# Attention and Fourier mixing on one core: the last of seven products moved into the next unit, and a fourth PSUM bank for products, taken from the attention scores

## The chip, the core and the metric

The kernel runs on one core of one Trainium2 chip. The metric is the device time of one execution in microseconds (us). The engines are named as in the profile: PE (matmuls) with PEld (its weight loads), DVE (vector), ACT (scalar and activation), POOL and SP (which issues most DMAs). Matmuls write to PSUM, which here holds eight banks, each 128 partitions x 512 fp32 values; ACT and DVE read the banks and write results to the larger on-chip memory.

## The reference

Two independent parts share one output, `out[:, :1024]` and `out[:, 1024:]`, with S = 2048 rows and D = 1024:

```
qkv = x @ wqkv                        # 32 heads of 32
scores = q k^T * 32**-0.5             # key allowed when 0 <= query - key < 256
a = softmax(scores) v @ wo
b = dft_seq_re @ (x2 @ dft_hid_re^T) - dft_seq_im @ (x2 @ dft_hid_im^T)
out = concat([a, b], axis=-1)
```

All of it is fp32. The kernel splits each fp32 operand into two fp16 parts, high and low, and multiplies in three passes (high x high, high x low, low x high).

## The kernel before, in words

**Units of seven products.** Every large matrix product is cut into units of 2 x 2 blocks, and a unit is computed with seven block products instead of eight, from sums and differences of blocks (`seven`). One product is 12 matmuls with 512 columns (four K tiles, three passes; for V 24 with 256 columns), issued in groups of four (`mm`, line 674). The seven use three PSUM banks a, b, c in the order a b a c a b a. The sums run on inside a bank: after product 1, ACT copies bank a to bank c (line 1123), product 3 adds to a and product 4 to the copy in c, and so on. After each of the products 2 to 7 ACT or DVE reads the bank: `keep` and `add_out` (lines 1198, 1201) and `halves_out` (lines 394, 402) in the projections, `copy` and `add` (lines 1375, 1378) in the Fourier part and in the output projection. PE may go on in a bank only when that reading is done. Banks a and b change places from unit to unit.

**Stages.** First come units for Q, K and V of one half of the rows (up to about 276 us in the profile), then those of the other half. From then on the attention runs beside them (`attention`, a generator that `tick` advances as matmuls are recorded). From about 500 us to 1590 us the attention runs beside the Fourier part, which alternates eight "x" units (hidden transform, two plain products in a bank of their own each) with eight "c" units of seven products (sequence transform). The output projection with `wo` stands last, from about 1640 us, again in units of seven.

**Operands of a unit.** `seven_parts` makes the left operands: three tiles `st`, each with two of the parts (products 1 and 4, 3 and 5, 2 and 7), and one part in a spare place (product 6). ACT writes the high half (line 1035) and DVE the low (line 1036). There are four `st` tiles, taken in turn. Sums on POOL or DVE (line 1014) come before.

**Attention.** A step `s_step` handles 128 queries of two heads. PE computes their scores against at most three key blocks of 128 into a tile `S` (line 546), of which there are two, two banks each, a head in a bank. The oldest and the newest block share one mask: DVE copies, by a triangular predicate, the oldest block's scores over the newest block's (line 552), so only two blocks go on. DVE takes the row maximum (556), POOL makes a bias (563), ACT exponentiates (566), ACT and DVE split into `hl` (395, 399), a DMA transposes to `t`, POOL masks `z` and `t` (581, 584), and `v_step` multiplies with V into the one bank `pv` (616). The same bank `pv` serves small transposes that spread a maximum over the partitions (lines 434 and 997, read by DVE in lines 436 and 999).

**What sets the order.** All operations are recorded first, with a cost and the buffers that they read and write (`Plan.op`, `Ring`). `Plan.run` then places them with a list scheduler: on each engine, the ready operation with the earliest due time. A due time follows from the order of PE operations in the recording. Each engine executes its list in that fixed order. A `Ring` with n buffers lets buffer k be written when all operations on buffer k-n are done; a ring marked `free` gives its buffers to whoever comes first.

Of the kernel before, what the change touches and what calls it, by code (L numbers as in the profile page):

```python
# [10 lines left out]
F32 = mybir.dt.float32  # L11
# [9 lines left out]
P = 128  # L21
# [275 lines left out]
def c_mm(n):  # L297
    return max(0.032, n / 2400.0 + 0.0025)
# [3 lines left out]
def fused_kernel(ctx: ExitStack, tc: tile.TileContext, xa, wqk, wv, wo, xb, wd, cs, out):  # L302
# [51 lines left out]
    banks = [Ring(R, lambda k, t=t: ps_m.tile([P, CH], F32, tag=f"m{t}", name=f"m{t}_{k}"), 1) for t in range(3)]  # L354
    s_ring = Ring(R, lambda k: ps_s.tile([P, 2, 512], F32, tag="s", name=f"s_{k}"), 2)
# [53 lines left out]
    def dve(cost, fn, r=(), w=(), port=False):  # L409
        op("DVE", cost, fn, r=r, w=w, port=port)  # L410
# [20 lines left out]
    def scale_of(key, v, s, wk, down=2.0 ** -14):  # L431
        t1 = tops.pop(key)
        pt = pv_ring.new()
        op("PE", 0.26, lambda: nc.tensor.transpose(pt.t[:, :P], t1.t[:, 0:1].to_broadcast([P, P]), ident),
           r=[(t1, 0), "ident"], w=[pt])
        dve(0.285, lambda: nc.vector.tensor_reduce(v, pt.t[:, :P], axis=AX.X, op=ALU.max), r=[pt], w=[wk])
# [53 lines left out]
    def attention():  # L490
# [33 lines left out]
        def s_step(b):  # L524
# [6 lines left out]
            mats, cost, keys = [], 0.0, []  # L531
            for j in range(2):
                h = 2 * hp + j
                k0 = qb + 1 - nb
                while k0 <= qb:
                    k1 = min(qb + 1, (k0 // QB + 1) * QB)
                    at = (k0 - (qb - 2)) * P
                    ku, qu = k2s[g, k0 // QB], q2s[g, sc]
                    keys += [(u, x) for u in (ku, qu) for x in range(3)]
                    mats.append((j, at, at + (k1 - k0) * P, qu, h, ku, k0 % QB * P, k0 % QB * P + (k1 - k0) * P))  # L540
                    cost += c_mm((k1 - k0) * P) + 0.01
                    k0 = k1

            def run():
                for j, a, e, qu, h, ku, ka, ke in mats:
                    nc.tensor.matmul(S.t[:, j, a:e], qu.t[:, h, i * P:i * P + P], ku.t[:, h, ka:ke],  # L546
                                     start=True, stop=True, skip_group_check=True)

            op("PE", cost, run, r=sorted(set(keys), key=lambda k: (k[0].k, k[1])), w=[(S, 0), (S, 1)])
            w = min(nb, 2) * P  # L550
            sv = lambda: S.t[:, :, 3 * P - w:3 * P]
            dve(0.425, lambda: nc.vector.copy_predicated(S.t[:, :, 2 * P:3 * P], upper2,  # L552
                                                         S.t[:, :, :P] if nb == 3 else never2),
                r=["upper", "never"], w=[(S, 0), (S, 1)])
# [415 lines left out]
    wps = banks[2].new()  # L970
# [13 lines left out]
    def u_look(n):  # L984
# [11 lines left out]
        pt = pv_ring.new()  # L996
# [107 lines left out]
    def bank():  # L1104
        nb[0] += 1
        return banks[nb[0] % 3].new()
# [9 lines left out]
    def seven(q, mats, ev, hook):  # L1116
        ring = {"a": banks[q % 2], "b": banks[1 - q % 2], "c": banks[2]}
        bk = {r: ring[r].new() for r in "abc"}
        for pos in range(7):
            ps = bk["abacaba"[pos]]  # L1120
            mm(ps, mats(pos))
            if pos == 0:
                op("ACT", 0.58, lambda: nc.scalar.activation(bk["c"].t, bk["a"].t, AF.Copy), r=[bk["a"]], w=[bk["c"]])  # L1123
            else:
                ev[pos](ps)
            hook(pos)
# [45 lines left out]
    def sum_unit(n, kd, gp, pr, how):  # L1172
# [37 lines left out]
        nseven[0] += 1  # L1210
        seven(nseven[0], mats, ev, lambda pos: qhook(n, pos))

    nseven = [0]
# [56 lines left out]
    at(where["v", 0, 1] - 2, 1, wv_fetch)  # L1270
# [9 lines left out]
    s2 = spots.index((where["v", 0, 1] + 2, 1))  # L1280
# [90 lines left out]
    def pair_of_tiles(q, lhs, rhs, y1, y2, f, fk, out_y, hook):  # L1371
# [9 lines left out]
        def last2(ps):  # L1381
            add(y2, 0, ps)
            out_y(2 * q + 1, y2)

        def last1(ps):
# [4 lines left out]
              4: lambda ps: add(y2, 1, ps), 5: last2, 6: last1}  # L1390
        seven(q, lambda pos: four(lhs[pos], lambda h, k: rhs(pos, h, k), pos < 2), ev, hook)
# [30 lines left out]
    def hook(n, turn):  # L1422
        for f, args in todo.pop((n, turn), ()):
            f(*args)
# [13 lines left out]
    for n, (kind, p, c, i) in enumerate(units):  # L1438
        rate[0] = late_rate * (RX if kind == "x" else 1.0)
        if kind == "x":  # L1440
            x = uns.pop(n)
# [24 lines left out]
        def out_y(t, y, p=p, c=c):  # L1466
# [3 lines left out]
            else:  # L1470
# [4 lines left out]
              lambda f=f: f.t, [f], out_y, lambda turn: hook(n, turn))  # L1475
    for q in range(NT // 2):
# [10 lines left out]

    for r in att_rings.values():
        r.after = turn_first
# [55 lines left out]
```

## Time and profile before

| | us |
|---|---|
| median of 3 runs | 1820.83 (1820.69 to 1822.73) |
| the profiled execution | 1815.42 |
| its span, first to last instruction | 1813.4 |
| PE busy | 1713.3 (94%) |
| DVE busy | 1349.6 (74%) |
| ACT busy | 1085.7 (60%) |
| POOL busy | 825.7 (46%) |

The profile comes from one execution. Rows of the groups read: line, engine, operation, out<-in with shapes, count, then busy time, mean ns of one, and the engine's idle time before them with what ended it. In the table of waits a row reads: who waited <- for whom: us in total, times, longest. Matmuls overlap in a pipeline, so the mean duration of one is longer than the step from one to the next.

### The profile page before, as it was taken

What the parts mean: (1) busy time and instruction counts of PE and PEld (TensorE: products, weight loads), DVE (VectorE), ACT (ScalarE), POOL (GpSimd) and SP (SyncE); (2) the same over time, 40 slices, a digit from 0 to 9 for tenths busy, and PEclk for the clock granted to TensorE, in tenths of its full rate; (3) what the DMA queues carried; (4) which work ended last, traced back from release to release, by engine and by line L of the source; (5) the groups of instructions that cost most, each with busy time, mean ns of one, the idle gap of its engine ahead of it and who ended that gap; (6) DMA issues with size and microseconds to landing.
All of it is one profiled execution on the core that took longest, in us unless ns stands there. A gap on an engine that the chain in (4) does not pass through costs nothing.

```text
span 1813.4 us, 31174 instructions
## 1 busy us (share of the span) xinstructions
PE 1713.3 (94%) x11286; PEld 893.2 (49%) x11286; DVE 1349.6 (74%) x2246; ACT 1085.7 (60%) x1718; POOL 825.7 (46%) x1018
## 2 busy tenths in 40 slices
PE   6999999999999989999989999988889999999998
PEld 2447587674444445444444445444445444444443
DVE  8879996666887887776887776886666778667641
ACT  3435635556666767766777767686556777563322
POOL 0124401324535565525676666766564767612000
PEclk8999999999999999999999999999999999999999
DMA  5586799999996688886599999579899659775331
GB/s 220 180 292 239 255 310 274 269 222 221 225 251 145 149 208 195 201 206 144 97 194 207 197 210 200 124 137 186 156 174 213 151 117 170 151 192 105 105 93 70
DMA packets 461274, 337.89 MB, mean 186 GB/s; under 512 B 340800, under 2 KB 411456, under 8 KB 461120
## 3 DMA queue, kind: packets, MB, share of 16 engines
q1 hardware_dynamic: 454208, 310.74, 70.7%
q0 software_dynamic: 6912, 25.17, 8.0%
q8 instruction: 88, 1.44, 0.3%
q14 instruction: 66, 0.54, 0.1%
HBM read 173.95 MB, written 88.47 MB: 145 GB/s over the span
## 4 chain that ended last, share of the span: by engine, by line
PE 42%; DVE 18%; POOL 11%; ACT 10%; issue 10%; DMA 8%; SPq 0%; POOLq 0%; DVEq 0%; ACTq 0%
PE m L674 38%; POOL raw L1014 3%; POOL bias L563 3%; DMA t<-hl 3%; ACT s L566 3%; DVE top L420 2%; DVE st L1036 2%; PE pv L616 2%; DVE hl L399 2%; ACT st L1035 2%; DVE mx L556 2%; PE s L546 2%; POOL z L581 2%; ACT hl L395 1%; POOL t L584 1%
## 5 line engine op out<-in xcount | busy, mean ns | idle before, releaser
L674 PE MATMUL m<-reg,st 128*128 128x512 f16 x4680 | 1105.7, 380 | 32.6 <-ACT m L1123 12.2
L674 PEld LDWEIGHTS <-st 128*128 128x128 f16 x5448 | 515.4, 98 | 614.0 <-issue 65.4
L566 ACT ACTIVATE s<-s,bias,escs 128x256 f32<-128x256 f32 (+1 forms) x512 | 271.0, 530 | 242.6 <-POOL bias L563 229.9
L563 POOL TENSOR_SCALAR bias<-mx,escs 128x2 f32<-128x2 f32 x256 | 124.8, 487 | 358.9 <-DVE mx L556 278.1
L399 DVE TENSOR_TENSOR hl<-s,hl 128x512 f16<-128x512 f32 (+1 forms) x256 | 171.3, 670 | 132.9 <-ACT hl L395 131.3
L1014 POOL TENSOR_TENSOR raw<-raw,raw 128x512 f32<-128x512 f32 x128 | 182.3, 1425 | 184.3 <-DVE st L1036 171.5
L581 POOL TENSOR_SCALAR_AFFINE_SELECT z<-t 128x512 f16<-128x512 f16 x224 | 177.6, 795 | 80.4 <-DMA t<-hl 61.5
L584 POOL TENSOR_SCALAR_AFFINE_SELECT t<-t 128x512 f16<-128x512 f16 x224 | 172.0, 771 | 11.1
L556 DVE TENSOR_REDUCE mx<-s 128x2 f32<-128x512 f32 (+1 forms) x256 | 170.4, 668 | 5.5 <-DVE o L627 0.3
L1036 DVE SCALAR_TENSOR_TENSOR st<-raw,sc,st 128x1024 f16<-128x1024 f32 x96 | 134.0, 1401 | 33.9 <-ACT st L1035 32.1
L674 PEld LDWEIGHTS <-reg 128*128 128x128 f16 x1212 | 116.6, 98 | 72.7 <-issue 7.8
L395 ACT ACTIVATE hl<-s 128x512 f16<-128x512 f32 (+1 forms) x256 | 148.0, 580 | 3.1 <-DMA t<-hl 0.2
L546 PE MATMUL s<-qk,qk 96*128 96x128 f16 (+2 forms) x704 | 120.8, 276 | 14.4 <-DVE hl L399 13.5
L674 PE MATMUL m<-xz,st 128*128 128x512 f16 x576 | 131.7, 384 | 2.3 <-DVE ybig L402 0.8
L1035 ACT ACTIVATE st<-raw,sc 128x1024 f16<-128x1024 f32 x96 | 109.5, 1143 | 31.4 <-PE m L674 14.6
L674 PE MATMUL m<-reg 128*128 128x512 f16 x480 | 124.2, 384 | 3.6 <-ACT reg L1375 3.6
L616 PE MATMUL pv<-vt,t 128*128 128x65 f16 x1984 | 114.6, 186 | 4.6 <-POOL t L584 3.9
L552 DVE COPY_PREDICATED s<-upper,s 128x256 f32<-128x256 uint32 x224 | 94.0, 420 | 32.9 <-PE s L546 32.1
L616 PEld LDWEIGHTS <-t 128*128 128x128 f16 x1984 | 96.1, 97 | 36.0 <-issue 4.8
L616 PE MATMUL pv<-vt,z 128*128 128x65 f16 (+1 forms) x896 | 99.2, 186 | 8.1 <-POOL z L581 5.3
L546 PEld LDWEIGHTS <-qk 96*128 96x128 f16 x704 | 61.9, 98 | 75.8 <-DVE hl L399 18.1
L616 PEld LDWEIGHTS <-z 128*128 128x128 f16 x896 | 81.3, 97 | 32.5 <-POOL z L581 7.0
(156 smaller groups left out, 2130.6 us busy)
## 6 DMA issues: line engine op xcount, KB each, us to landing
raw<-in_cs_dram SPq DMA_DIRECT2D x64, 512.0 KB, 4.7
raw<-in_xb_dram SPq DMA_DIRECT2D x48, 512.0 KB, 5.3
qk<-qs SPq DMA_DIRECT2D x192, 128.0 KB, 3.8
out_dram<-ybig POOLq DMA_DIRECT2D x36, 512.0 KB, 7.9
qs<-ybig SPq DMA_DIRECT2D x64, 256.0 KB, 4.4
raw<-in_wd_dram SPq DMA_DIRECT2D x32, 512.0 KB, 4.9
raw<-in_wqk_dram SPq DMA_DIRECT2D x22, 512.0 KB, 5.6
vs<-ybig SPq DMA_DIRECT2D x32, 260.0 KB, 4.7
```

The costliest lines, as they stand in the source:

```text
L395: else nc.scalar.activation(dst(), src(), AF.Copy), r=r, w=w)
L399: op("DVE", c_dve(n), lambda: nc.vector.tensor_tensor(dst(), src(), hi(), op=ALU.subtract), r=r, w=w, port=port)
L546: nc.tensor.matmul(S.t[:, j, a:e], qu.t[:, h, i * P:i * P + P], ku.t[:, h, ka:ke], start=True, stop=True, skip_group_check=True)
L556: dve(c_dve(2 * w), lambda: nc.vector.tensor_reduce(mx.t, sv(), axis=AX.X, op=ALU.max, negate=True), r=[(S, 0), (S, 1)], w=[mx])
L563: op("POOL", 0.215, lambda: nc.gpsimd.tensor_scalar(bias.t, mx.t, es, PSHIFT, op0=ALU.mult, op1=ALU.add), r=[mx, ("esc", g // 2)], w=[bias])
L566: op("ACT", 0.32 + 0.00085 * w, lambda h=h: nc.scalar.activation(sv()[:, h], sv()[:, h], AF.Exp, bias=bias.t[:, h:h + 1], scale=es), r=[bi ...
L581: op("POOL", 0.637, lambda: nc.gpsimd.affine_select(out=z.t, in_=pk(), compare_op=ALU.is_gt, fill=0.0, base=0, pattern=[[0, 4], [-1, P]], ...
L584: op("POOL", 0.637, lambda: nc.gpsimd.affine_select(out=pk(), in_=pk(), compare_op=ALU.is_ge, fill=0.0, base=0, pattern=[[0, 4], [1, P]], ...
L616: nc.tensor.matmul(pvt()[:, r, j, lo:], lhs, vt.t[:, k % QB, at + lo:at + VW], start=a, stop=e, skip_group_check=True)
L674: nc.tensor.matmul(ps.t[:, j * n:j * n + n], lhs(), rhs(), start=first, stop=last, skip_group_check=True)
L1014: lambda: e.tensor_tensor(o(), a(), b(), op=ALU.subtract if sub else ALU.add), r=r, w=w, port=True)
L1036: op("DVE", c_dve(n, True), lambda: nc.vector.scalar_tensor_tensor(dst(1), src(), scl(), dst(0), op0=ALU.mult, op1=ALU.subtract), r=[*r, s ...
```

## The change

Each unit now uses banks in the order a b (a of the unit before) a b c a: products 1 and 2, then product 7 of the unit before (`flush`), then 3, 6, 4, 5. Product 7 is kept back as `last_of` until the next unit, so a unit's bank a lives into the next one and there are two banks a in turn. That makes four banks for products: two for a, one for b, one for c. Between two products in one bank stand two others, as recorded. In the Fourier part and the output projection the two additions into `y2` change places accordingly. `flush` is also called where the kind of work changes (before the second half, before "x" units, before and after the output projection).

The fourth bank comes from the scores. A tile `S` now is one bank and holds the two newer key blocks of both heads. The oldest block's scores go to a new bank `old`, of which there is one. The small transposes use `old` in place of `pv`. The score matmuls of a step become two recorded operations, `S` first, then `old`. The program has 352 more matmuls (11638 for 11286).

```diff
-    banks = [Ring(R, lambda k, t=t: ps_m.tile([P, CH], F32, tag=f"m{t}", name=f"m{t}_{k}"), 1) for t in range(3)]
-    s_ring = Ring(R, lambda k: ps_s.tile([P, 2, 512], F32, tag="s", name=f"s_{k}"), 2)
+    a_ring, b_ring, c_ring = (Ring(R, lambda k, t=t, n=n: ps_m.tile([P, CH], F32, tag=f"m{t + k % n}", name=f"m{t + k % n}_{k}"), n)
+                              for t, n in ((0, 2), (2, 1), (3, 1)))
+    old_ring = Ring(R, lambda k: ps_v.tile([P, CH], F32, tag="old", name=f"old_{k}"), 1, free=True)
+    s_ring = Ring(R, lambda k: ps_s.tile([P, 2, 2 * P], F32, tag="s", name=f"s_{k}"), 2)
...
     def scale_of(key, v, s, wk, down=2.0 ** -14):
-        pt = pv_ring.new()
+        pt = old_ring.new()
...
+            old = old_ring.new() if nb == 3 else None
...
+            n2 = min(nb, 2)
+            scores(lambda j, a, e: S.t[:, j, (2 - n2 + a) * P:(2 - n2 + e) * P], qb + 1 - n2, qb + 1, [(S, 0), (S, 1)])
+            if old is not None:
+                scores(lambda j, a, e: old.t[:, j * P:j * P + P], qb - 2, qb - 1, [old])
+            w = n2 * P
+            sv = lambda: S.t[:, :, 2 * P - w:2 * P]
+            dve(0.425, lambda: nc.vector.copy_predicated(
+                S.t[:, :, P:2 * P], upper2,
+                old.t[:, :2 * P].rearrange("p (j k) -> p j k", j=2) if nb == 3 else never2),
+                r=["upper", "never"] + ([old] if nb == 3 else []), w=[(S, 0), (S, 1)])
...
-        return banks[nb[0] % 3].new()
+        return (a_ring, b_ring, a_ring, c_ring)[nb[0] % 4].new()
...
-    def seven(q, mats, ev, hook):
-        ring = {"a": banks[q % 2], "b": banks[1 - q % 2], "c": banks[2]}
-        bk = {r: ring[r].new() for r in "abc"}
-        for pos in range(7):
-            ps = bk["abacaba"[pos]]
+    def flush():
+        if last_of[0] is not None:
+            last_of[0]()
+            last_of[0] = None
+
+    def seven(mats, ev, hook):
+
+        a, b, c = a_ring.new(), b_ring.new(), c_ring.new()
+        mm(a, mats(0))
+        op("ACT", 0.58, lambda: nc.scalar.activation(c.t, a.t, AF.Copy), r=[a], w=[c])
+        hook(0)
+        mm(b, mats(1))
+        ev[1](b)
+        hook(1)
+        flush()
+        hook(2)
+        for turn, (pos, ps) in enumerate(((2, a), (5, b), (3, c), (4, a))):
             mm(ps, mats(pos))
-            if pos == 0:
-                op("ACT", 0.58, lambda: nc.scalar.activation(bk["c"].t, bk["a"].t, AF.Copy), r=[bk["a"]], w=[bk["c"]])
-            else:
-                ev[pos](ps)
-            hook(pos)
+            ev[pos](ps)
+            hook(3 + turn)
+
+        def last():
+            mm(a, mats(6))
+            ev[6](a)
+
+        last_of[0] = last
...
-    at(where["v", 0, 1] - 2, 1, wv_fetch)
+    at(where["v", 0, 1] - 2, 3, wv_fetch)
...
     for n, (kd, gp, pr, how) in enumerate(plan):
         if n == half1:
+            flush()
...
         def last2(ps):
-            add(y2, 0, ps)
+            add(y2, 1, ps)
             out_y(2 * q + 1, y2)
...
-              4: lambda ps: add(y2, 1, ps), 5: last2, 6: last1}
+              5: lambda ps: add(y2, 0, ps), 4: last2, 6: last1}
...
         if kind == "x":
+            flush()
```

The scheduler decides what stands where. Three places in PE's list follow; tiles m0 to m3 are the product banks, and the rows left out at "..." are the weight loads and the other matmuls of a group of four. First, the output projection near the end, where product 5 has just ended in m0 and product 7 needs it. Before:

```order
L674 MATMUL m0_84_19998<-ext_18971,st_185_19885 128x512
L674 LDWEIGHTS raw_219_19767
L674 MATMUL m1_85_20042<-ext_18971,raw_219_19767 128x512
...
L674 LDWEIGHTS st_186_19922
L674 MATMUL m0_84_19998<-ext_18971,st_186_19922 128x512 [waits DVE_49]
```

The same place now, where product 7 of m0 follows groups of the next unit in m1 and m2:

```order
L683 MATMUL m0_96_20458<-ext_19552,st_183_20357 128x512
L683 LDWEIGHTS raw_218_20340
L683 MATMUL m1_97_20570<-reg2_82,raw_218_20340 128x512
...
L683 MATMUL m2_78_20586<-reg2_82,st_186_20526 128x512 [waits DVE_49]
...
L683 LDWEIGHTS raw_218_20340
...
L683 LDWEIGHTS st_184_20410
L683 MATMUL m0_96_20458<-ext_19552,st_184_20410 128x512 [waits DVE_49]
```

Before, one group of four matmuls stood between the two users of m0; now there are four groups, 16 matmuls.

Second, a turn from one c unit to the next. The tile st_102 takes the place of st_98 and is filled when the last product on st_98 has ended. Before, from that product to the first on st_102:

```order
L674 MATMUL m0_47_11496<-reg1_81,st_98_11434 128x512
...
L674 MATMUL m1_48_11576<-reg1_81 128x512
...
L674 MATMUL m0_47_11496<-reg1_81,st_99_11477 128x512 [waits DVE_49]
...
L674 MATMUL m1_49_11779<-reg1_81,st_100_11599 128x512 [waits DVE_49]
...
L674 MATMUL m0_48_11881<-reg1_81,st_102_11765 128x512 [waits Activation_49]
```

And now:

```order
L683 MATMUL m1_55_11648<-reg1_81,st_98_11646 128x512
...
L625 MATMUL pv_69_11971<-vt_18_11293,z_107_11933 128x65
...
L683 MATMUL m0_56_11948<-reg1_81,st_100_11870 128x512
...
L683 LDWEIGHTS st_102_11984 [waits Activation_49]
L683 MATMUL m2_45_12027<-reg1_81,st_102_11984 128x512
...
L683 LDWEIGHTS st_102_11984 [waits DVE_49]
```

Before, 28 matmuls of 512 columns and a PV step stood between the two; now it is 8 and a PV step.

Third, the scores around the same place. Before, both matmuls of a step and a transpose in `pv`:

```order
L546 LDWEIGHTS qk0_18_10965 [waits DVE_49]
L546 MATMUL s_147_11799<-qk1_20_11393,qk0_18_10965 128x384 [waits PE_49]
L546 LDWEIGHTS qk0_18_10965
L546 MATMUL s_147_11799<-qk1_20_11393,qk0_18_10965 128x384
L997 MATMUL pv_104_11804<-ident_85,topone_36_11712 128x128 [waits DVE_49,PE_49]
```

Now, with two steps' matmuls into `old`, the second of which waits for DVE to have read the first:

```order
L549 MATMUL s_145_12008<-qk1_20_11732,qk0_18_11380 128x256 [waits DVE_49]
...
L549 MATMUL old_145_12013<-qk1_19_11116,qk0_18_11380 128x128 [waits DVE_49]
...
L549 MATMUL old_146_12046<-qk1_20_11732,qk0_18_11380 128x128 [waits DVE_49]
...
L549 MATMUL s_146_12085<-qk1_20_11732,qk0_18_11380 128x256 [waits Activation_49]
```

One matmul of 384 columns has become one of 256 and one of 128 in another bank, and the step's two parts may stand in either order.

More of the change, by code (lines that the diff above doesn't have):

```diff
@@ L530, in s_step @@
             d = st[b] = {}
[L531 to L554, printed above, removed]
+            old = old_ring.new() if nb == 3 else None
@@ new lines, in scores, with run @@
+            def scores(dst, k0, k_end, w):
+                mats, cost, keys = [], 0.0, []
+                for j in range(2):
+                    h, k = 2 * hp + j, k0
+                    while k < k_end:
+                        k1 = min(k_end, (k // QB + 1) * QB)
+                        ku, qu = k2s[g, k // QB], q2s[g, sc]
+                        keys += [(u, x) for u in (ku, qu) for x in range(3)]
+                        mats.append((j, k - k0, k1 - k0, qu, h, ku, k % QB * P, k % QB * P + (k1 - k) * P))
+                        cost += c_mm((k1 - k) * P) + 0.01
+                        k = k1
+                def run():
+                    for j, a, e, qu, h, ku, ka, ke in mats:
+                        nc.tensor.matmul(dst(j, a, e), qu.t[:, h, i * P:i * P + P], ku.t[:, h, ka:ke],
+                                         start=True, stop=True, skip_group_check=True)
+                op("PE", cost, run, r=sorted(set(keys), key=lambda k: (k[0].k, k[1])), w=w)
@@ L968, in warm_up @@
         op("PE", n * 0.3, run, r=[("R", 40)], w=[ps])
-    wps = banks[2].new()
+    wps = c_ring.new()
     for i in range(4):
@@ L995, in u_look @@
         t1 = tops.pop(key)
-        pt = pv_ring.new()
+        pt = old_ring.new()
         op("PE", 0.26, lambda: nc.tensor.transpose(pt.t[:, :P], t1.t[:, 0:1].to_broadcast([P, P]), ident),
@@ L1209, in sum_unit @@
               6: lambda ps: plain_out(ps, 0, 1)}
-        nseven[0] += 1
-        seven(nseven[0], mats, ev, lambda pos: qhook(n, pos))
-    nseven = [0]
+        seven(mats, ev, lambda turn: qhook(n, turn))
     def x_piece(pr, r):
@@ L1279, in fused_kernel @@
             at(*spots[s1 + 2 * i + 3], scan_scale, key)
-    s2 = spots.index((where["v", 0, 1] + 2, 1))
+    s2 = spots.index((where["v", 0, 1] + 2, 3))
     for e in range(2):
@@ L1389, in pair_of_tiles @@
         ev = {1: lambda ps: copy(y2, 1, ps), 2: lambda ps: copy(y2, 0, ps), 3: lambda ps: copy(y1, 0, ps),
-              4: lambda ps: add(y2, 1, ps), 5: last2, 6: last1}
-        seven(q, lambda pos: four(lhs[pos], lambda h, k: rhs(pos, h, k), pos < 2), ev, hook)
+              5: lambda ps: add(y2, 0, ps), 4: last2, 6: last1}
+        seven(lambda pos: four(lhs[pos], lambda h, k: rhs(pos, h, k), pos < 2), ev, hook)
     todo = {}
@@ L1440, in fused_kernel @@
         if kind == "x":
+            flush()
             x = uns.pop(n)
@@ L1486, in fused_kernel @@
               lambda: fo, ["fo"], out_o, lambda turn: None)
+    flush()
     for r in att_rings.values():
```

2 lines of the change are left out of this document (added).

## The prediction

> **What bounds the kernel now.** I read the busy shares first, then the stretches, then who PE waited for, because the change moves PE's matmuls and who frees their banks.
>
> ```profile
> span 1813.4 us, 31174 instructions
> PE 1713.3 (94%) x11286; PEld 893.2 (49%) x11286; DVE 1349.6 (74%) x2246; ACT 1085.7 (60%) x1718; POOL 825.7 (46%) x1018
> ...
> PE 42%; DVE 18%; POOL 11%; ACT 10%; issue 10%; DMA 8%; SPq 0%; POOLq 0%; DVEq 0%; ACTq 0%
> ```
> ```profile
> 0.00:318.00 318.00, 294.58 (x1883) 181.59 (x1884) 268.17 (x348) 146.47 (x193) 71.58 (x87) 0.98 0.77 253
> 318.00:520.00 202.00, 196.54 (x1466) 113.39 (x1464) 151.98 (x274) 121.56 (x208) 76.55 (x118) 1.00 0.97 235
> 520.00:1590.00 1070.00, 1014.32 (x7002) 505.86 (x7000) 813.31 (x1496) 739.74 (x1221) 659.20 (x799) 0.99 0.84 172
> 1590.00:1813.00 223.00, 207.86 (x944) 92.41 (x942) 116.13 (x130) 77.96 (x99) 18.41 (x16) 0.99 0.44 115
> ```
> PE is busy 93 to 97% in every stretch (columns: PE, PEld, DVE, ACT, POOL, clock, DMA) at a granted clock of 0.98 to 1.00, no other engine above 85%. So time is won only where PE stands still, 100 us in all, and lost wherever PE is made to stand. These are the waits of PE (total us, times, longest):
>
> ```profile
> PE m L674 <- ACT m L1123: 14.4, 16, 2.0
> PE s L546 <- DVE hl L399: 13.5, 16, 1.7
> ...
> PE m L674 <- DVE ybig L1378: 7.5, 9, 3.5
> PE m L674 <- ACT ybig L1375: 6.4, 1, 6.4
> PE pv L616 <- POOL z L581: 5.3, 2, 4.1
> PE m L674 <- DVE late L1378: 4.3, 5, 1.5
> ...
> PE pv L616 <- POOL t L584: 3.9, 6, 1.6
> PE pv L997 <- DVE o L627: 3.7, 4, 2.1
> PE m L674 <- ACT reg L1375: 3.6, 1, 3.6
> PE m L674 <- ACT reg L1198: 3.3, 3, 1.9
> PE m L674 <- DVE reg L1201: 2.8, 5, 0.8
> PE m L674 <- DVE ybig L402: 2.4, 6, 0.5
> PE m L674 <- ACT ybig L394: 1.6, 1, 1.6
> PE pv L616 <- DVE vwd L436: 1.3, 2, 1.0
> PE m L674 <- DVE st L1036: 1.3, 3, 0.6
> PE pv L616 <- DVE o L627: 1.3, 3, 0.8
> ...
> PE m L674 <- DVE reg L1378: 1.0, 3, 0.4
> PE pv L616 <- DVE sc L999: 0.8, 3, 0.4
> ...
> PE pv L434 <- DVE sc L999: 0.3, 1, 0.3
> ```
> Ten of these rows (m behind L1123, L1375, L1378, L1198, L1201, L402 and L394) are one thing: a product wants a bank that ACT or DVE has not finished reading. They sum to 47.3 us in 50 waits. One such place, near the end:
>
> ```profile
> 1746.69 1.03 PE L674 MATMUL m<-ext,st 128*128 128x512 f16 x4
> ...
> 1747.55 1.03 PE L674 MATMUL m<-ext,raw 128*128 128x512 f16 x4
> ...
> 1748.06 1.23 DVE L1352 TENSOR_TENSOR late<-raw 128x1024 f32<-128x1024 f16 x1 [8.63 <-DMA raw<-ots]
> ...
> 1749.20 1.40 DVE L1378 SCALAR_TENSOR_TENSOR late<-m,fo,late 128x512 f32<-128x512 f32 x2
> 1749.99 1.02 PE L674 MATMUL m<-ext,st 128*128 128x512 f16 x4 [1.42 <-DVE late L1378]
> ```
> Four matmuls start every 0.86 us (1746.69 to 1747.55), 0.216 us each, yet are shown busy for 1.03: the last overhangs by 0.17. An idle time thus hides about 0.17 us of the delay, and the 50 waits cost 47.3 + 8.5 = 55.8 us. Here the evicting add stood behind another DVE instruction that waited for a DMA, and PE had only one group of four matmuls to run meanwhile.
>
> **1. Two products between users of a bank.** Counted over the whole order, each matmul at its step in the trace: of 500 turnarounds (a matmul needs a bank that ACT or DVE must first read) 255 have under 2.5 us of PE's work in between; in the changed kernel 100 of 499. The waits of the trace lie almost all in that class, since an eviction takes 0.58 to 0.75 us and the rest is its queue. If those that stay close wait as often as now, 55.8 x 100/255 = 21.9 us stay and 33.9 us go. Upper end: all 55.8. Lower end: 20, because the two single waits of 6.4 and 3.6 us show ACT late by more than one further product (12 x 0.216 = 2.6 us) covers, and the shorter rows may lose less than their share. I take 34, the count being the nearest thing to a measurement. The copy of the first product into the third bank (16 waits, 14.4 us) is part of it: both its reader's wait and its writer now have two or more products.
>
> **2. The score bank.** The third key block goes to its own bank, of which there is one, and which the transposes of scales now use too. PE may write the next one only when DVE's masking copy has read the last.
>
> ```profile
> L552 DVE COPY_PREDICATED s<-upper,s 128x256 f32<-128x256 uint32 x224 | 94.0, 420 | 32.9 <-PE s L546 32.1
> ```
> The copy itself stays one of 0.42 us. The trace has no such bank; the nearest is the single bank pv, which DVE also frees and which PV steps and transposes share today. Its rows (L997 behind o, L616 behind vwd, o and sc, L434 behind sc) are 7.4 us in 13 waits, 9.6 us with the overhang, at 177 reuses of which 26 have under 2 us of PE's work between. After: pv has 7 such, the new bank 55 of 273. At 9.6/26 = 0.37 us each, 62 cost 22.9, so 13 us more than now. Ends: 10 us gained if none waits; 25 lost if half of the 62 wait at the 1.1 us that a bank wait costs today (55.8/50). I take 13. Behind a wait of PE here stand its products, and ACT and DVE behind those. The score tile keeps two buffers, so the 13.5 us behind the `hl` subtraction stay: counted from the later of both matmuls, reuses under 8 us go from 76 to 98, but those from 8 to 12 from 156 to 140.
>
> **3. Parts of a unit stay longer.** Product 7 reads the part that product 2 reads, and product 5, now the last before the next unit, the part that product 3 reads. There are four such tiles (`st`), so the next unit's second part is filled only after product 5, with little more than its first product to cover it.
>
> ```profile
> L1036 DVE SCALAR_TENSOR_TENSOR st<-raw,sc,st 128x1024 f16<-128x1024 f32 x96 | 134.0, 1401 | 33.9 <-ACT st L1035 32.1 <-POOL t L584 1.3
> ...
> L1035 ACT ACTIVATE st<-raw,sc 128x1024 f16<-128x1024 f32 x96 | 109.5, 1143 | 31.4 <-PE m L674 14.6
> ```
> A fill is 1.14 us on ACT and then 1.40 on DVE, 2.5 in a row. Of 185 refills 3 have under 5 us of PE's work between today, and 27 in the changed kernel, 16 of these under 4. PE waits for such a fill 1.3 us in all today. A close reuse of a bank costs 55.8/255 = 0.22 us now, and a fill passes two queues, so 0.44 x 24 = 10.5 us. Ends: 0, as the slack is still positive everywhere, and 26 (24 x 1.1). I take 10.5. The few units whose parts are loaded by SP's queue are in the 27. ACT's queue stands behind such a fill: exponentials wait there, but PE has two score tiles.
>
> **4. Shorter score matmuls.** The changed program has 352 more matmuls and weight loads in 176 blocks; columns stay the same.
>
> ```profile
> 1003.38 0.50 PE L546 MATMUL s<-qk,qk 96*128 96x128 f16 x4 [0.30 <-DVE hl L399]
> 1003.72 1.89 PE L674 MATMUL m<-reg,st 128*128 128x512 f16 x8
> ...
> 1009.78 0.50 PE L546 MATMUL s<-qk,qk 96*128 96x384 f16 x2 [0.71 <-DVE hl L399]
> 1010.11 0.20 PE L616 MATMUL pv<-vt,z 128*128 128x65 f16 x1
> ...
> L546 PEld LDWEIGHTS <-qk 96*128 96x128 f16 x704 | 61.9, 98 | 75.8 <-DVE hl L399 18.1
> ```
> A block in four matmuls (128 and 256 columns) takes 0.34 us to the next instruction, one in two of 384 takes 0.33. So 176 x 0.01 = 1.8 us. Lower end 0; upper end, if each of the 448 matmuls of 128 columns had to stand for its weight load (98 ns against about 55 by those 0.34 us), 19. I take 1.8, since the split block exists in the trace.
>
> The Trainium skill, "TensorE: Matmul & The Clock Gate", section "Back-to-back issue gap", gives a sustained spacing of about 81 ns for 128-column matmuls in a stream of load and matmul pairs. By that the 448 would take an estimated 11.6 us more than at 55 ns, and the sum would come out near no change. The trace does not agree: two matmuls of 256 and two of 128 in 0.34 us leave no room for 81.
>
> **5. Hooks, y tiles, ends.** Hooks keep seven places a unit; the fetch of the V weights moves from hook 1 to hook 3 of its unit, still two units ahead of its reader. Output tiles live about three products longer, four tiles against two a unit. Nothing for either. At the very end the last product follows its bank's last reader directly, as it does before.
>
> **Sum.** -33.9 + 13 + 10.5 + 1.8 = -8.6 us. Profiled: 1815.42 us, of which the span is 1813.4; the median of the runs, 1820.83, lies 5.4 above it, and I carry that over: span 1804.8, median 1812.
>
> **Rivals.** (a) The new waits stay covered, as the planner places other products in these gaps: terms 2 and 3 near 0, so -32 us and 1789. For it: the fills cause 1.3 us now; against: the gaps before were also placed by the planner and 50 of them failed. (b) Slower: the single score bank takes over. DVE is 76% busy from 520 to 1590 and works in order; with a 1.2 to 1.4 us fill ahead of the masking copy, PE stands. It decides from 0.56 us for each of the 62 close reuses (34.7 less 9.6 is 25 us, which with terms 3 and 4 outweighs the 33.9 by over 0.2%); at 0.7 us it is 33.8 lost, +12 and 1833. Against it: 0.37 in the nearest row. (c) Slower too: the late refill, 1.1 us at each of the 24: +7 and 1828. (d) Each 128-column matmul stands for its weight load: 19 for 1.8, +9 and 1830. Against it stands the 0.34 us; the section of the Trainium skill named under 4 speaks for a part of it. (e) No change: 55.7 of PE's 100 idle us lie between 520 and 1590 (1070.0 less 1014.3), where scores and masks follow a chain over four engines; if 9 us of what PE gains there become longer waits behind `hl`, `z` and `t` (22.7 us today), -8.6 becomes 0: 1821. That the order doesn't do what it says is excluded by the 255 and 100.
>
> **Chances.** Forecast 0.46, (a) 0.16, (e) 0.14, (b) 0.14, (c) 0.07, (d) 0.03. Three runs of this kernel spread by 0.1%, so 0.2% (3.6 us) is about what can be told from no change. Faster: 0.46 + 0.16 = 0.62; same 0.14; slower 0.24. The likeliest case alone has 1802 to 1817. The range runs from (a), 1789, to 1832, which takes in (c) and (d) and about half of (b).
>
> **What would show it.** Right: PE's waits for m behind ACT and DVE near 19 us (22 with overhang); waits of the new tile `old` and of pv together near 20; m behind `st` fills near 10; score blocks at 0.34 us; the stretches before 318 and after 1590, where no score bank exists and few refills are close, shorter by some 5 us each of the 23.4 and 15.1 us that PE idles there (318.0 less 294.58, 223.0 less 207.86). Wrong: bank waits that stay above 35 us (ACT and DVE late by more than two products), more than 35 us on `old` and pv, or waits behind `hl`, `z` and `t` that grow by more than 10.

## The result, and the profile after

| | before | after |
|---|---|---|
| median, us | 1820.76 (1819.67 to 1822.73) | 1771.78 (1766.37 to 1774.66) |
| profiled execution, us | 1815.42 | 1771.06 |

The two were run four times each on the same chip. The ratio is 0.9726, with a 95% interval of 0.9701 to 0.9751: the changed kernel is 49 us faster. The prediction said 1812 with a range of 1789 to 1832, so the direction was right and the size far off; the time lies 17 us below the range.

First the span, the busy times and the engines' shares of the chain of waits, in the profile of after:

```profile
span 1769.4 us, 31787 instructions
PE 1700.2 (96%) x11638; PEld 909.5 (51%) x11638; DVE 1347.5 (76%) x2246; ACT 1086.2 (61%) x1718; POOL 825.1 (47%) x1018
...
PE 56%; DVE 11%; POOL 10%; ACT 9%; issue 8%; DMA 6%; SPq 0%; POOLq 0%; DVEq 0%; ACTq 0%
```

The span fell by 44.0 us, PE's busy time by only 13.1 (1713.3 to 1700.2), and that of the other engines hardly: PE stands idle 69.2 us where it stood 100.1. In the chain, PE's share went from 42% to 56%, DVE's from 18% to 11%: the end is now set more by PE itself.

The same stretches of after (us, busy us of PE, PEld, DVE, ACT, POOL with counts, clock, DMA share, GB/s):

```profile
0.00:318.00 318.00, 299.32 (x1927) 185.55 (x1928) 269.19 (x351) 149.25 (x199) 73.60 (x89) 0.98 0.77 254
318.00:520.00 202.00, 199.97 (x1499) 117.22 (x1498) 157.69 (x280) 124.81 (x211) 75.90 (x115) 1.00 1.00 246
520.00:1590.00 1070.00, 1027.48 (x7419) 528.53 (x7416) 825.40 (x1512) 756.01 (x1237) 665.72 (x806) 1.00 0.85 178
1590.00:1769.00 179.00, 173.39 (x802) 78.21 (x800) 95.27 (x105) 56.09 (x74) 9.88 (x8) 0.99 0.38 97
```

PE's idle time is less in each: 18.7 us for 23.4 before 318, 2.0 for 5.5, 42.5 for 55.7 between 520 and 1590, and 5.6 for 15.1 after 1590, a stretch that now holds 802 matmuls for 944. The waits of PE (us in total, times, longest):

```profile
PE s L549 <- DVE hl L401: 16.3, 21, 2.0
...
PE m L683 <- ACT reg L1400: 4.7, 2, 3.6
PE pv L625 <- POOL t L593: 4.2, 5, 1.3
PE m L683 <- DVE st L1045: 4.1, 3, 1.8
PE m L683 <- ACT m L1136: 4.0, 8, 1.2
PE m L683 <- DVE reg L1227: 3.2, 3, 2.4
PE old L549 <- DVE s L560: 2.0, 2, 1.4
PE pv L625 <- POOL z L590: 1.8, 2, 1.6
PE pv L625 <- DVE o L636: 1.7, 4, 0.7
PE m L683 <- DVE ybig L1403: 1.3, 3, 0.7
...
PE m L683 <- ACT ybig L1400: 1.2, 1, 1.2
PE old L1006 <- DVE s L560: 0.8, 2, 0.4
PE m L683 <- DVE late L1403: 0.8, 1, 0.8
...
PE m L683 <- DVE reg L404: 0.5, 1, 0.5
PE old L549 <- DVE vwd L441: 0.5, 1, 0.5
PE old L436 <- DVE s L560: 0.4, 1, 0.4
...
PE pv L625 <- DVE sc L1012: 0.3, 1, 0.3
...
PE m L683 <- ACT reg L1224: 0.2, 1, 0.2
```

The rows of a product that wants its bank back (m behind L1400, L1136, L1227, L1403, L404, L1224) sum to 15.9 us in 20 waits, where there were 47.3 in 50. The waits of `old` and pv behind DVE sum to 5.7 us in 11; before, pv alone had 7.4 in 13. The refills of `st` cost 4.1 us in 3 waits, before 1.3 in 3.

**All of PE's lost time by cause.** The gaps alone don't sum to the 44 us. For every matmul I took the step from its start to the next matmul's start, less the ordinary step of its form (216 ns for 512 columns), and put the excess down to what released the next one; a slow step with no wait stands by itself. This counts the 0.17 us that a gap hides, and the slow clock. To see past the luck of one order, I averaged kernels that do equal work in another order, got by changing one cost constant of the scheduler (below): three of before, three with only the score side of the change, four of after. In us:

| what PE lost time to | before | score side only | after | after less before | predicted |
|---|---|---|---|---|---|
| bank of a product not read yet | 55.7 | 52.7 | 19.0 | -36.7 | -33.9 |
| slow matmuls without a wait | 21.4 | 13.3 | 12.8 | -8.6 | none |
| pv behind POOL's `z`, `t` | 13.0 | 4.4 | 7.4 | -5.6 | none |
| banks pv and `old` not read yet | 10.6 | 12.6 | 11.5 | +0.9 | +13 |
| parts and other operands late | 2.9 | 3.6 | 4.1 | +1.2 | +10.5 |
| scores behind `hl` | 18.7 | 20.4 | 21.2 | +2.5 | none |
| excess of short matmuls | 1.8 | 2.5 | 2.7 | +0.9 | +1.8 |
| mean span | 1817.0 | 1802.9 | 1773.1 | -43.9 | -8.6 |

The rows of the last column but one sum to -45.4; rows left out (the start, 13.9 us in each) make up the rest. The profiled execution of before lay 5.3 us under its median, that of after 0.7, which is why the medians differ by 49 and the profiled executions by 44.4.

### The profile page after: what moved, and what is told of

The parts are those of the page before. It is cut to its first block, busy times and chain, and to the rows that moved or that the text cites. A ratio compares the mean times of both kernels' runs of the same rounds, so it can differ in the third digit from the quotient of the medians.

```text
span 1769.4 us, 31787 instructions
## 1 busy us (share of the span) xinstructions
PE 1700.2 (96%) x11638; PEld 909.5 (51%) x11638; DVE 1347.5 (76%) x2246; ACT 1086.2 (61%) x1718; POOL 825.1 (47%) x1018
## 4 chain that ended last, share of the span: by engine, by line
PE 56%; DVE 11%; POOL 10%; ACT 9%; issue 8%; DMA 6%; SPq 0%; POOLq 0%; DVEq 0%; ACTq 0%
PE m L683 51%; POOL raw L1023 4%; ACT s L575 3%; POOL bias L572 2%; DMA raw<-in_cs_dram 2%; PE pv L625 2%; DVE hl L401 2%; DVE st L1045 2%; PE s L549 2%; POOL t L593 1%; DVE mx L565 1%; DMA t<-hl 1%; POOL z L590 1%; ACT hl L397 1%; ACT st L1044 1%
## 5 line engine op out<-in xcount | busy, mean ns | idle before, releaser
L683 PE MATMUL m<-reg,st 128*128 128x512 f16 x4680 | 1110.8, 379 | 14.1 <-ACT reg L1400 4.7
L572 POOL TENSOR_SCALAR bias<-mx,escs 128x2 f32<-128x2 f32 x256 | 129.0, 504 | 375.0 <-DVE mx L565 327.4
L1023 POOL TENSOR_TENSOR raw<-raw,raw 128x512 f32<-128x512 f32 x128 | 188.6, 1474 | 156.4 <-DVE st L1045 121.2
L590 POOL TENSOR_SCALAR_AFFINE_SELECT z<-t 128x512 f16<-128x512 f16 x224 | 170.7, 767 | 63.1 <-DMA t<-hl 43.7
L593 POOL TENSOR_SCALAR_AFFINE_SELECT t<-t 128x512 f16<-128x512 f16 x224 | 175.6, 791 | 10.1
L1045 DVE SCALAR_TENSOR_TENSOR st<-raw,sc,st 128x1024 f16<-128x1024 f32 x96 | 133.5, 1393 | 21.5 <-ACT st L1044 20.9
L549 PEld LDWEIGHTS <-qk 96*128 96x128 f16 x1056 | 93.4, 97 | 108.9 <-issue 30.8
L560 DVE COPY_PREDICATED s<-upper,old 128x256 f32<-128x256 uint32 x224 | 94.3, 421 | 45.7 <-PE old L549 31.5
L549 PE MATMUL s<-qk,qk 96*128 96x128 f16 (+1 forms) x608 | 96.2, 252 | 17.9 <-DVE hl L401 16.3
L422 DVE TENSOR_REDUCE top<-raw 128x1 f32<-128x1024 f32 x72 | 85.9, 1207 | 14.1 <-DMA raw<-in_xa_dram 4.7
```

Source lines behind the costliest of these rows:

```text
L549: nc.tensor.matmul(dst(j, a, e), qu.t[:, h, i * P:i * P + P], ku.t[:, h, ka:ke], start=True, stop=True, skip_group_check=True)
L572: op("POOL", 0.215, lambda: nc.gpsimd.tensor_scalar(bias.t, mx.t, es, PSHIFT, op0=ALU.mult, op1=ALU.add), r=[mx, ("esc", g // 2)], w=[bias])
L590: op("POOL", 0.637, lambda: nc.gpsimd.affine_select(out=z.t, in_=pk(), compare_op=ALU.is_gt, fill=0.0, base=0, pattern=[[0, 4], [-1, P]], ...
L593: op("POOL", 0.637, lambda: nc.gpsimd.affine_select(out=pk(), in_=pk(), compare_op=ALU.is_ge, fill=0.0, base=0, pattern=[[0, 4], [1, P]], ...
L683: nc.tensor.matmul(ps.t[:, j * n:j * n + n], lhs(), rhs(), start=first, stop=last, skip_group_check=True)
L1023: lambda: e.tensor_tensor(o(), a(), b(), op=ALU.subtract if sub else ALU.add), r=r, w=w, port=True)
```

## The experiments

**The kernel again, and other orders of the same work.** The scheduler places operations by costs; a tiny change of one constant gives another order of the same instructions. In each of before, after and the kernel with the score side alone, `WIRE` was changed in one run, as shown, and `SEM` (0.034 to 0.036) in another:

```diff
-WIRE = 2.0
+WIRE = 2.02
```

> The changed kernel itself, unaltered, beside the three halves of the change on one chip: 1767 to 1776 us by every theory (1771.8 was its median, 1820.8 that of the kernel before). It fixes the scale for the other three.

> The kernel before, with one number of the planner's model changed (the landing time that it assumes for a DMA, 2.00 to 2.02 us). Instructions, banks and buffers are the same; some 30% of the places in the engines' lists change, 261 close bank turnarounds against 255. Theory L (the scores alone won 15 to 18 us because their other order happens to avoid the long stalls at 1245 to 1300 us and the half-clock stretches after them, and any other order might): a time of its own, anywhere between 1800 and 1830. Theory C (freeing pv and splitting the scores really pays 15): 1821 within 4.

> The kernel before with another number of the model changed (the semaphore's time, 0.034 to 0.036 us); 10% of the places in the lists change, 260 close bank turnarounds. Theory L: again a time of its own between 1800 and 1830. Theory C: 1821 within 4.

> The changed kernel with 2.02 us for 2.00 in the planner's model; over 30% of the places change, 110 close bank turnarounds against 100. If the change's gain is systematic and not one lucky order: 1765 to 1782. If the changed kernel was a lucky order: 1785 or more.

> The changed kernel with 0.036 us for 0.034 in the planner's model; some 40% of the places change, 102 close bank turnarounds. Systematic gain: 1765 to 1782. Lucky order: 1785 or more.

Measured against before on the same chip: after again 1769.07 us (0.973 [0.9696, 0.9764]); before with `WIRE` 1811.83 (0.9965 [0.9945, 0.9986]), with `SEM` 1815.71 (1.0011 [0.9989, 1.0033]); after with `WIRE` 1774.64 (0.9766 [0.9742, 0.9789]), with `SEM` 1780.81 (0.9808 [0.9783, 0.9833]). So an order is worth up to 0.8%, and the change's own order is the best of its three by 7 to 14 us (0.973 against 0.9766 and 0.9808). The worst order of after still beats the best of before by 1.6%. The mean ratios are 0.9992 for before and 0.9767 for after: some 41 us of the 49 belong to the change, the rest to its order.

**The score side alone.** Before with the banks `S` and `old`, the split scores and the transposes in `old`, but three product banks in the old order:

```diff
-    s_ring = Ring(R, lambda k: ps_s.tile([P, 2, 512], F32, tag="s", name=f"s_{k}"), 2)
+    old_ring = Ring(R, lambda k: ps_v.tile([P, CH], F32, tag="old", name=f"old_{k}"), 1, free=True)
+    s_ring = Ring(R, lambda k: ps_s.tile([P, 2, 2 * P], F32, tag="s", name=f"s_{k}"), 2)
...
-        pt = pv_ring.new()
+        pt = old_ring.new()
```

> The kernel before with three product banks and the old order, and only the scores changed: S in one bank, the oldest block and the small transposes in the new bank old, 352 more matmuls; one PSUM bank stays unused. 250 close bank turnarounds (255 before), 46 close reuses of old and 7 of pv against 26 of pv. Theory S: nothing to win or lose, 1821 within 4. The recorded prediction's terms for the score bank and the shorter matmuls (13 and 1.8 us): 1836. Rival P (the freed pv bank and the split are what pays): 1800 or less.

> The kernel with only the scores changed, with 2.02 for 2.00 us in the planner's model; 253 close bank turnarounds against 250. Theory L (its 0.9917 was partly a lucky order; equal orders of the kernel before gave 0.9965 and 1.0011): near 1.0, 1812 to 1825. Theory C (splitting the scores and freeing pv pays some 15 us whatever the order): 0.988 to 0.995, 1799 to 1811. The prediction's +15: 1836.

> The kernel with only the scores changed, with 0.036 for 0.034 us in the planner's model; 257 close bank turnarounds. Theory L: 1812 to 1825. Theory C: 1799 to 1811. The prediction's +15: 1836.

1802.58 us, 0.9917 [0.9887, 0.9947]; the other two orders 1801.54 (0.9893 [0.9857, 0.9929]) and 1808.59 (0.9937 [0.9912, 0.9962]). The part that I had priced at a loss of 13 + 1.8 gains 14 us (a mean ratio of 0.9916, against 0.9992 for the three orders of before). Its waits show where:

```profile
PE pv L624 <- DVE o L635: 5.3, 8, 1.3
...
PE old L548 <- DVE s L559: 1.6, 3, 0.8
...
PE pv L624 <- POOL t L592: 0.9, 2, 0.5
...
PE pv L624 <- POOL z L589: 0.8, 1, 0.8
```

Score matmuls wait 1.6 us for the single bank `old` behind the masking copy. All rows of `old` after the start sum to 4.9 us and those of pv behind DVE to 5.6, against 7.4 on pv alone before, so the gain is not there. The waits of pv behind `z` and `t`, 9.2 us before, are 1.7.

**A fourth bank, without the move.** The changed kernel with its banks and scores, but the seven products in the order a b a c a b a again, product 7 in its own unit:

```diff
-        for turn, (pos, ps) in enumerate(((2, a), (5, b), (3, c), (4, a))):
+        for pos in range(7):
+            ps = (a, b, a, c, a, b, a)[pos]
...
-        last_of[0] = last
```

> Four product banks and the new scores, but the old order of the seven products (a b a c a b a, product 7 in its own unit); only bank a changes between two from unit to unit. Counted in the order, 142 of 499 bank turnarounds have under 2.5 us of PE's work in between (255 before, 100 in the changed kernel). Theory S (the distance between users of a bank is what pays): the change won 49 us for 155 fewer close turnarounds, 0.32 us each with all that follows, so 113 fewer give -36: 1785 us. Rival B (the fourth bank alone pays): 1772. Rival M (only the move of product 7 pays): 1821. Rival P (the score split pays, products hardly matter): near 1772.

1778.95 us, 0.9775 [0.9738, 0.9812]. Beside the 1802.58 of the score side alone, on the same chip, the fourth bank alone gains 24 us: units alternate between two banks a, so a unit starts in a bank that the unit before did not use. Turnarounds with under 2.5 us of PE's work between fall from 250 to 142 (100 with the move), and the bank waits come out at 20.2 us, as in after (20.1). The two longest of its rows, of a product that wants its bank back:

```profile
PE m L683 <- ACT m L1134: 9.2, 12, 1.8
...
PE m L683 <- DVE reg L1388: 2.6, 2, 1.8
```

Beside it after has 1769.07 us on this chip: the move on top gains 10 us in this pair (8 by the ratios), less than the spread of the orders, and 1 to 2 us against the mean of after's orders (0.9767). So its own share is not settled.

**The new order, without the move.** After with `flush()` at the end of each unit: products 1, 2, 3, 6, 4, 5, 7.

```diff
         last_of[0] = last
+        flush()
```

> The changed kernel with product 7 kept in its own unit: order 1 2 3 6 4 5 7, so product 7 follows product 5 in the same bank directly, with two banks a in turn. 158 close bank turnarounds, 5 close refills of st (27 in the changed kernel). Theory S: 97 fewer than before at 0.32, -31: 1790 us. Rival B (fourth bank alone): 1772. Rival M (the move alone pays): 1821. If refills of st cost what the prediction said (10.5 us), this kernel gets them back: 1780.

1785.57 us, 0.9818 [0.9789, 0.9847]. 158 close turnarounds and 25.2 us of bank waits. Its profiled span is 15 us longer than after's: 5 are bank waits, the other 10 stand behind `hl` (27.5 us for 21.4) and in slow matmuls (16.1 for 10.8).

**Old scores in the bank pv.** To make the reuse of one bank dense, as I had feared it, `old` was put into pv together with PV steps and transposes; one bank stands unused.

```diff
-    old_ring = Ring(R, lambda k: ps_v.tile([P, CH], F32, tag="old", name=f"old_{k}"), 1, free=True)
...
+    old_ring = pv_ring
```

> The changed kernel, but the oldest block's scores and the small transposes go to the bank pv, beside the PV steps; one PSUM bank stays unused. The suspected cost of term 2 is made large: 401 buffers take turns in one bank that DVE frees, 243 of them with under 2 us of PE's work in between (55 on old and 7 on pv in the changed kernel). At the prediction's 0.37 us for each close reuse: +67, about 1838. At the 0.12 us that the changed kernel's trace shows (7.5 us at 62): +22, about 1793. If DVE is never late there: 1771.

1811.51 us, 0.9955 [0.9937, 0.9973]: some 40 us more than after, between the expectations. Of 401 reuses of pv 243 have under 2 us of PE's work between, against 7 in after. Waits of this kernel:

```profile
PE s L549 <- DVE hl L401: 24.6, 29, 8.0
...
PE pv L549 <- DVE o L636: 5.1, 11, 1.0
...
PE pv L1006 <- DVE o L636: 2.9, 4, 2.1
...
PE pv L625 <- DVE s L560: 1.6, 4, 0.5
```

Delays at pv itself, 21.5 us by the measure of the table, are 12 more than on pv and `old` in after, for 181 more close reuses (243 for 55 + 7): 0.07 us each, where the prediction took 0.37. The larger part lies elsewhere: behind `hl` (32.6 us for 21.4) and in slow matmuls (26.1 for 10.8). Part of it is the transposes, which also go to pv here: with them alone in pv (below, 0.9839) the kernel is some 21 us faster than this one.

**A third score tile.** If the waits behind `hl` and at pv came from too few score tiles, the unused bank should mend them:

```diff
-    s_ring = Ring(R, lambda k: ps_s.tile([P, 2, 2 * P], F32, tag="s", name=f"s_{k}"), 2)
+    s_ring = Ring(R, lambda k: ps_s.tile([P, 2, 2 * P], F32, tag="s", name=f"s_{k}"), 3)
```

> As the kernel with old in pv, with the freed bank given to a third score tile S. PE's longest wait in the changed kernel is for S behind the hl subtraction (16.3 us, 21 times, some 20 with what the pipeline hides). With three tiles that goes: 15 to 20 us less than the kernel with old in pv. If sharing pv costs nothing this is 1752; at 0.12 us a close reuse 1775; at 0.37 us about 1820.

1812.49 us, 0.9967 [0.9934, 1.0]: no gain over the kernel above, against an expected 15 to 20. The waits moved rather than went; these are its rows (its profiled execution, 1821.69 us, lies 9 us above its median):

```profile
PE s L549 <- DVE hl L401: 21.1, 14, 7.9
...
PE pv L625 <- POOL z L590: 9.8, 5, 2.9
...
PE pv L625 <- POOL t L593: 6.7, 8, 2.2
```

Behind `z` and `t` PE now waits 16.5 us (5.0 in the kernel above). So nothing shows the number of score tiles to be the limit; that theory found no support.

**The transposes back in pv.** The score side alone, and the whole change, each with the small transposes returned to pv, at both places:

```diff
-        pt = old_ring.new()
+        pt = pv_ring.new()
```

> The kernel with only the scores changed, with the small transposes back in the bank pv: old holds the oldest block's scores alone. 28 close reuses of pv (31, 26 and 29 in three orders of the kernel before, 5 to 7 with the scores changed), 19 of old. Theory V (the 15 us of the scores come from taking the transposes out of pv): near the kernel before, 1812 to 1822. Rival W (they come from the scores' own bank and split): 1800 to 1809, as with the scores changed.

> The changed kernel with the small transposes back in pv, old for scores alone: 99 close bank turnarounds, 23 close reuses of pv, 20 of old. Theory V: some 12 to 15 us more than the changed kernel's orders (1769 to 1781): 1782 to 1795. Rival W: 1769 to 1781.

The score side with it: 1814.94 us, 0.9986 [0.9953, 1.0019]; without it the ratio was 0.9917. So, as far as one order tells, splitting the scores between two banks is worth nothing that can be told, and moving the transposes out of pv is the whole gain of that part, 12 us here; the ratio lies outside those of the score side's three orders (0.9893 to 0.9937). The whole change with it: 1786.67 us, 0.9839 [0.9799, 0.9879], against 0.973: 20 us, or 13 against the mean of after's orders (0.977). Both hit what was expected of the transposes. But the waits at pv did not show it: in the second kernel the banks pv and `old` cost 8.3 us by the table's measure, in after 9.3. What grew most is one row,

```profile
PE s L549 <- DVE hl L401: 26.5, 31, 4.7
```

which was 16.3 us in 21 waits. The half clock grew too: after the start, PE does 14.8 us of its work at half the clock there and 3.4 in after, which is 5.7 us more lost.

**Made stalls.** The table's second row needs a cause. In after, six places in the output projection were given a stall: PE writes a small tile, DVE reduces it, then makes one (first kernel) or four (second) more reductions of 1.2 us that nothing needs, and the products wait for the end of them.

```diff
+            nc.vector.tensor_reduce(c.t, pt.t[:, :P], axis=AX.X, op=ALU.max)
+            for _ in range(k):
+                nc.vector.tensor_reduce(c.t, ybig[:, 0].rearrange("p e c -> p (e c)"), axis=AX.X, op=ALU.max)
...
+        if 1 <= q <= 6:
+            stall(1)
```

> The changed kernel with six made stalls of PE in the output projection, where no attention runs: a transpose, one DVE reduction of 1024 columns that waits for it and a second transpose that waits for the reduction, before units 2 to 7. Each stops PE for some 1.9 us (0.28 + 1.21 and the hand-overs): about 12 us in all, 1782 beside 1770. Theory H (a wait costs more than itself only where the clock falls to half after it): no half-clock stretches there, so the stalls cost their own length.

> As the kernel with short stalls, with four reductions in a row: each stops PE for some 5.5 us, 33 us in all by their own length, 1803 beside 1770. Theory H: half-clock stretches of 3.4 to 6.8 us follow at least some of them, each costs a further 1.7 to 3.4 us, so 1808 to 1820 with the clock below 0.99. Against it: 1803 and no such stretches.

1792.97 us (0.9857 [0.9813, 0.9902]) with short stalls, 1823.3 (1.0018 [0.9988, 1.0048]) with long ones, both above what was expected. The waits and the stretch of the stalls, of the kernel with short ones and then of that with long ones:

```profile
PE old L688 <- DVE topone L685: 13.1, 6, 2.2
1640.00:1830.00 190.00, 135.68 (x611) 60.57 (x611) 63.96 (x75) 34.99 (x48) 0.00 (x0) 0.97 0.24 71
```
```profile
PE old L688 <- DVE topone L685: 35.7, 6, 6.0
1640.00:1830.00 190.00, 147.81 (x610) 63.74 (x608) 79.71 (x87) 35.37 (x48) 0.00 (x0) 0.89 0.22 64
```

The same matmuls are busy 12.1 us longer behind the long stalls, at a granted clock of 0.89 for 0.97. After one of them:

```profile
1720.86 0.47 PE L688 MATMUL old<-ident,topone 128*128 128x128 f32 x1 [5.95 <-DVE topone L685]
1721.13 1.91 PE L699 MATMUL m<-reg,raw 128*128 128x512 f16 x4
1722.83 1.91 PE L699 MATMUL m<-reg,st 128*128 128x512 f16 x4
1724.54 1.91 PE L699 MATMUL m<-reg,raw 128*128 128x512 f16 x4
1726.25 1.16 PE L699 MATMUL m<-reg,st 128*128 128x512 f16 x4
1727.24 1.03 PE L699 MATMUL m<-reg,raw 128*128 128x512 f16 x4
```

Groups of four follow each other at 1.71 us, 0.43 a matmul, until 1726.25, and from 1727.24 (the next starts at 1728.11) at about 0.86 again. The clock's own records show 0.5 for 6.83 us around the end of each of the six long stalls, and for 3.41 us after two of the six short ones. The long stretch at 0.5 begins 1.1 to 1.6 us before its stall ends, so that 5.3 to 5.7 us of it fall on matmuls: a stall of 6 us costs some 2.8 us more than it lasts. The two profiled spans differ by 29.2 us (1823.0 and 1793.8): 22.6 of waits and 12.1 of busy time, less 5.5 won elsewhere. The profile with short stalls has 20.5 us at half clock besides the start and the end, 17.1 more than that of after. PE works in 18.4 of them, 9.2 us lost for 1.7 in after; the 7.5 us between, with the 13.1 of waits, are 20.6 of the 24.4 us by which its span is longer than after's. Only 6.83 of the 20.5 us follow the stalls; the others stand elsewhere, in an order that these edits change too.

## Why the prediction was wrong

**Term 1, two products between users of a bank, was right.** Predicted -33.9, measured -36.7 (-31.4 in the gap rows). The scaling by close turnarounds, 255 to 100, gave 21.9 us left; 20.1 were left in the profiled run, 19.0 in the mean. It foretold the stretch before 318 too: 4.7 us less idle for some 5. But the move is less of it than the text of the prediction implied: the fourth bank alone had nearly the same bank waits (20.2).

**Term 2, the score bank, has the wrong sign (+13).** Here the largest part of the miss arose. It priced each close reuse of `old` at 0.37 us, taken from pv. In the profiled run `old` has 55 close reuses, which cost 3.5 us in all, 0.06 each; `old` and pv together are +0.9 us in the table. With the rest of its change the score side did not lose 13 + 1.8 us but gained 14. A close reuse costs only when the queue that must free the bank is late, and pv's price held the lateness of PV steps' readers, not that of the masking copy, which in after takes what it always took:

```profile
L560 DVE COPY_PREDICATED s<-upper,old 128x256 f32<-128x256 uint32 x224 | 94.3, 421 | 45.7 <-PE old L549 31.5
```

The prediction also let the transposes leave pv as a gain of the 26 to 7 close reuses alone, a few us inside the 13. The two kernels with the transposes back in pv show 12 to 20 us. The gain lies not in direct waits for pv, but behind `z`, `t` (13.0 to 4.4 us in the score-side kernels) and in slow matmuls (21.4 to 13.3). That these follow from transposes standing between PV steps is argued: the link between them was not shown. The profile of the score side with the transposes back in pv bears it out only in part: 4.8 us behind `z` and `t`, against 1.7 without them and 9.2 in before.

**Term 3, late parts (+10.5), did not come.** 27 refills have little of PE's work to cover them, as counted, but these 27 cost 0.3 us; the row of `st` grew by 2.8 us, the mean by 1.2. The slack that the text called "still positive everywhere" was the right reading, its price from another class of waits the wrong one. Here too a count of close places was multiplied by a price that came from places where the other engine is late.

**Term 4 (+1.8) was about right: +0.9.** The score matmuls of the changed kernel:

```profile
1013.62 0.38 PE L549 MATMUL s<-qk,qk 96*128 96x256 f16 x2
1013.84 0.27 PE L549 MATMUL old<-qk,qk 96*128 96x128 f16 x2
...
1016.57 0.27 PE L549 MATMUL old<-qk,qk 96*128 96x128 f16 x2
1016.68 1.03 PE L683 MATMUL m<-reg,st 128*128 128x512 f16 x4
```

Two of 256 columns take 0.22 us to the next start, two of 128 take 0.11: 0.33 together, as the pair of 384 did. Rival (d) is out. The spacing of about 81 ns for 128 columns that the Trainium skill ("TensorE: Matmul & The Clock Gate", section "Back-to-back issue gap") gives is not seen here: it is 55 ns, with a weight load each.

**Missing: the clock after a long wait (-8.6).** The prediction read "0.98 to 1.00" as a clock at full speed. In before, the wait of 6.38 us that it quotes stands ahead of this:

```profile
1247.78 3.57 PE L674 MATMUL m<-reg,st 128*128 128x512 f16 x8 [6.38 <-ACT ybig L1375]
...
1251.66 1.89 PE L674 MATMUL m<-reg,st 128*128 128x512 f16 x8
```

Eight matmuls in 3.4 us to the next start, against 1.73 for the next eight. Five such stretches, 27.3 us at half the clock, lie in that execution, and PE works in 21.1 us of them, so 10.5 us are lost; they follow waits of 6.4 (`ybig`), 4.1 and 1.6 (`z`, `t`), 3.6 (`reg`), 2.1 (`o`), and 1.7 and 0.8 us (`hl`, m). After has one of 3.41 us, behind the `reg` wait of 3.6 us. The cores' rows, before and after, carry it:

```profile
core 0: 1813.4 us, clock 0.988
```
```profile
core 0: 1769.4 us, clock 0.995
```

In the mean of before's three profiles 13.6 us are lost so after the start, in the score side's 4.3, in after's four 3.9: the fall of 9.7 us accounts for all of the row of slow matmuls in the table (-8.6). Over all runs, span times (1 - clock), which counts the start, and idle time at half clock too, is 21.9 us in 78 runs of before, 11.7 in 8 of after, 14.1 to 15.5 in the orders with the score side alone, 17.8 and 15.6 in the two with transposes back in pv, 31.5 with long stalls. So a long wait that goes was worth up to some 3 us more than its row, and the loss is there at other places as well.

**The range.** Rival (a), which ended it at 1789, set the new waits to zero but gave neither the clock nor the transposes a gain. The 0.2% that the prediction took, from three runs, for what can be told was too little as well: the 78 runs of before, on four chips, lie between 1808.8 and 1831.3 us. Term by term the miss of 36.8 us (-45.4 for -8.6) is: bank waits -2.8, score banks -12.1, refills -9.3, short matmuls -0.9, clock -8.6, `z` and `t` -5.6, `hl` +2.5. Rivals (b), (c), (e) are out: `old` never became the bound, refills were in time, and `hl`, `z` and `t` together did not grow in the mean.

**Open.** Why transposes in pv cost 12 to 20 us that don't show as waits for pv, and how much the move itself brings beside the fourth bank: on one chip 10 us against the old order with four banks, 16 against its own order without the move, one order of each, with orders that scatter by up to 14.

## What to carry to other kernels

A count of close reuses gives a good forecast only with a price from the same pair of engines: what matters is whether the queue that frees the buffer is late there, and a short copy at the head of its queue costs little even at a close reuse (0.06 us here). Read the granted clock around each long wait, not its mean over a stage: a wait of two us or more may be followed by half-speed matmuls. And before crediting a gain to a change in a scheduled kernel, run a few other orders of the same work; here they differ by up to 0.8%.

## What the runs showed of the hardware

The half clock comes in whole lengths. After the start, and but for the last stretch, which the end cuts off, the clock's records of all 18 kept profiles show 0.5 for 3.41 or 6.83 us, and in two cases, around waits of 8.0 and 7.9 us, for 10.24. Six waits of 6 us brought 6.83 us each; six of 2.2 us brought 3.41 us twice and nothing four times. The Trainium skill ("TensorE: Matmul & The Clock Gate", section "🔬 Part 1: The HAM clock gate (the "warmup" mystery)") has PE watched in windows of about 3.4 us that run freely, and the clock halved after an idle one; the lengths agree. That waits shorter than a window already do it in some places, as the 2.1-us wait behind `o` and the short stalls do here, is more than that section says.

The profiles show what decides. In each, all changes of the clock lie on one grid of 3.413 us, to within 2 ns. Cut into these intervals, the 18 profiles (without the first 30 us and the end) have 9182 at full clock, and 73 of them are followed by half clock: by the profile's busy times, all 56 in which PE stood idle for 62% (2.1 us) or more, 17 of 64 between 48 and 62%, and none of the 9062 below. So a wait of 2.2 us halves the clock or not by where it falls: the two short stalls that did so lay within one interval with 2.16 and 2.19 us, the other four were cut by its edge, with 1.95 us of the wait at most in one. Of 100 intervals at half clock the 27 in which PE idled for over 19% were followed by another, the other 73 were not; behind the long stalls the first is idle for 33 to 46%, so that there are two.

The 78 runs of before show what this does to the spread: 14 runs at a mean clock of 0.989 have a mean span of 1813.4 us, 12 at 0.986 have 1821.0. A clock lower by 0.003 is 5.5 us of PE's work lost in a span of 1817, most of those 7.6 us. Over all 78 runs, span times (1 - clock) goes with 60% of the variance of the spans: the runs of one kernel differ for a good part in how often its waits bring the half clock.
